# Attention and its end in another order: next pair converted first, reciprocals later, broadcasts behind the tail scores, the first batch's root in three steps

## The chip, the cores and the metric

The kernel runs on one core of one Trainium2 chip. The metric is the device time of one execution in microseconds (us). The kernel before the change took 605.54 us (median of 3 runs, 603.80 to 607.98).

The core's engines run side by side, each through its own list of instructions in order: TensorE (PE, matrix products), VectorE (DVE), ScalarE (ACT), GpSimd (POOL) and SyncE (SP), which issues most transfers (DMA). They meet at semaphores only: an instruction that waits holds up everything behind it on its engine.

## The reference, cut to what matters

Attention with a soft cap, then two gated layers. Every matrix product is made in pieces of higher and lower halves of the operands (`hi`/`lo`), since the result is float32.

```python
# q, k, v: (2 batches, 12 heads, 448 rows, 64 columns)
scores = cap * tanh(matmul(q, k.T) / sqrt(64) / cap)
attn = exp(scores - max(scores))
attn = attn / (sum(attn) + 1e-9)
x = matmul(attn, v)                      # -> (896, 768), heads side by side
rms = sqrt(mean(x * x) + 1e-6)
xn = x / rms * rms_g
h = silu(xn @ w_gate) * (xn @ w_val)     # 768 -> 1536
y = h @ w_out                            # 1536 -> 768
z = y @ w_in                             # 768 -> 2048
out = (max(z, 0) + alpha * min(z, 0)) @ w_out2
```

## The kernel before, in words

The 24 heads are taken as 12 pairs (0 to 5 are the first batch, 6 to 11 the second). A pair is worked on in two bursts of scores, so there are 24 bursts, 0 to 23: burst 2i holds the score groups 0 and 1 of pair i, burst 2i + 1 the groups 2 and 3. For each burst, a list written out by hand gives this order: PE makes the scores (`qk`, L189), ACT takes tanh and exp of them (`soft`, L199 and L201), PE multiplies the preceding burst's exp with V (`pv`, L212), and then come the steps that `at(n, ...)` has hung on this burst, in the order in which they were hung. Every step puts its instructions at the end of its engines' lists. The score banks in PSUM are two, so scores of a burst wait for the tanh of the one before.

The steps that the change touches are:

- `prep` (L175, L176): DVE splits the next pair's Q and K into `hi` and `lo`. `load_raw` and `load_v`: SP issues the loads of a later pair. The tiles for each of them are two.
- `sums` (L228): PE adds up exp over the keys into `us`. `evac_o` (L254) and `evac_u` (L262): DVE copies O and these sums out of PSUM; four small transfers (L267) then spread the sums over partitions (`gt`).
- `recip` (L276 to L287): for two pairs together, DVE makes the reciprocals of the sums in four small instructions, and SP issues two transfers (L287) of their halves `th` and `tl` into rows `r`.
- `norm` (L312, L313): PE broadcasts such a row over the partitions (one matmul into `rps`), and DVE multiplies O by it. `square` (L294 to L302): POOL, or ACT in the last pairs, squares the result and POOL adds the squares up.
- `rms` (L331 to L335): PE sums the squares of a batch over the partitions (`ms`), ACT takes the root, DVE the reciprocal. `xnorm` (L348 to L354): DVE scales a tile by it and, in the first batch, splits it into halves.
- `w_top`, `w_bits`, `w_hi`, `w_lo` (L103, L107, L120, L124): ACT and DVE unpack a weight tile and split it. `sum1` to `sum4` (L115): POOL adds weight tiles. Eight weight tiles are unpacked within the attention.
- `sums_now`, `norm_now`: the same sums and norm for the last pair, without the transfers.
- `product` (L366) and `products` (L378): PE's weight products. Directly behind the attention stand the first four products (`A11` with `B11`, `A12` with `B21`, each for the weight groups 0 and 1, two rows of nine matmuls each), with the rest of the normalisation between them; then the second weight stage begins with `products` into the bank `m`.

In the kernel before, the root of the first batch is one step: root on ACT, reciprocal on DVE, and the weight casts of the same burst behind both. The long rest of the program (the seven products of each weight block, their sums, the second layer) has a list of its own, which the change leaves alone but for one subtraction.

## Time and profile before

| what | value |
|---|---|
| three runs | 603.80, 605.54, 607.98 us |
| profiled execution | 603.23 us, of which the span of the trace is 601.5 us |
| PE busy | 574.0 us, 95% of the span, 2925 matmuls |
| DVE busy | 387.1 us, 64% |
| ACT busy | 340.5 us, 57% |
| POOL busy | 110.1 us, 18% |
| transfers | 66.05 MB, mean 110 GB/s |
| granted clock, mean | 0.994 of full speed |

PE is busy nearly all the time, but not evenly: in the first 150 us there are slices with six to nine tenths, and one whose granted clock is below full speed. The share is an average over stages; what a change in one stage is worth is read from that stage. Names such as `s<-hi,lo` in the rows mean output tile and input tiles. "x8" means that eight instructions stand in one row, and `[4.19 <-ACT pt L199]` that the engine was idle for 4.19 us before the row, until ACT's instruction of L199 on tile `pt`.

### The profile page before, as it was taken

How to read it: one execution, taken by the hardware profiler on the slowest of the kernel's cores; microseconds unless marked ns; L12 is line 12 of the kernel's file. 1: busy time of each engine (PE TensorE's matmuls, PEld its weight loads, DVE VectorE, ACT ScalarE, POOL GpSimd, SP SyncE). 2: the span in 40 equal slices, each digit the busy share in tenths (PEclk: the TensorE clock that was granted, in tenths of full speed). 3: DMA queues.
4: the chain of work that ended last, by engine and by line, in shares of the span. 5: the costliest groups of instructions: out<-in, count | busy, mean ns of one | idle time of the engine just before them, and what ended most of it. 6: DMA issues, size and time to landing. Idle time of an engine off the chain costs nothing.

```text
span 601.5 us, 7318 instructions
## 1 busy us (share of the span) xinstructions
PE 574.0 (95%) x2925; PEld 473.2 (79%) x2925; DVE 387.1 (64%) x428; ACT 340.5 (57%) x389; POOL 110.1 (18%) x60
## 2 busy tenths in 40 slices
PE   6989996999899999999999999999989999999997
PEld 3434332467789999999999999999989889999996
DVE  4546767959899777758861555989986877604100
ACT  6898867834836446347362543686775977323101
POOL 0001550234005524510000035400451000000000
PEclk9999999899999999999999999999999999999999
DMA  7553432040033543313433563003331344431002
GB/s 256 178 175 113 150 103 69 3 158 1 1 106 122 161 146 114 141 53 105 163 134 125 170 244 112 0 1 109 134 125 53 111 152 157 158 129 69 1 1 92
DMA packets 17166, 66.05 MB, mean 110 GB/s; under 512 B 4204, under 2 KB 4716, under 8 KB 17132
## 3 DMA queue, kind: packets, MB, share of 16 engines
q1 hardware_dynamic: 16844, 65.45, 31.6%
q8 instruction: 23, 0.38, 0.2%
q0 software_dynamic: 144, 0.13, 0.1%
q14 instruction: 11, 0.09, 0.0%
q10 hardware_dynamic: 144, 0.00, 0.0%
HBM read 62.66 MB, written 2.75 MB: 109 GB/s over the span
## 4 chain that ended last, share of the span: by engine, by line
PE 74%; DVE 16%; ACT 4%; DMA 3%; issue 2%; SPq 1%; ACTq 0%; DVEq 0%
PE s L366 18%; PE m L366 15%; PE s L633 6%; PE s L629 6%; PE s L631 6%; PE m L629 5%; PE m L633 5%; PE m L631 5%; PE oo L212 2%; DVE b L542 2%; PE s L189 2%; DVE lo L176 2%; DMA gt<-us 2%; DVE wt L107 1%; PE m L378 1%
## 5 line engine op out<-in xcount | busy, mean ns | idle before, releaser
L124 DVE TENSOR_TENSOR wl<-wt,wh 128x768 fp32r<-128x768 f32 x98 | 108.4, 1111 | 94.3 <-ACT wh L120 93.2
L115 POOL TENSOR_TENSOR wt<-wt 128x768 f32<-128x768 f32 x40 | 91.6, 2296 | 250.4 <-DVE wt L107 144.9
L120 ACT CAST wh<-wt 128x768 fp32r<-128x768 f32 x98 | 81.3, 833 | 93.0 <-PE s L631 22.1
L103 ACT CAST top<-raw 128x768 f16<-128x768 bf16 x68 | 72.6, 1076 | 48.3 <-DVE wt L107 40.8
L107 DVE SCALAR_TENSOR_TENSOR wt<-raw,top 128x768 uint32<-128x768 uint32 x68 | 68.2, 1006 | 0.0
L366 PE MATMUL s<-xh,wh 128*128 128x448 f32 x222 | 57.5, 368 | 0.9 <-DVE b L542 0.9
L366 PE MATMUL s<-xl,wh 128*128 128x448 f32 x222 | 57.2, 366 | 0.8 <-DVE xl L542 0.8
L366 PE MATMUL s<-xh,wl 128*128 128x448 f32 x222 | 57.1, 366 | 0.0
L629 PE MATMUL s<-ks,wh 128*128 128x448 f32 x176 | 50.4, 366 | 1.1 <-DVE b L870 1.1
L633 PE MATMUL s<-ks,wl 128*128 128x448 f32 x176 | 50.3, 365 | 0.0
L199 ACT ACTIVATE pt<-s,cinv 128x896 f32<-128x896 f32 (+1 forms) x48 | 41.1, 905 | 12.4 <-PE s L189 12.2
L366 PE MATMUL m<-xh,wh 128*128 128x448 f32 x174 | 45.0, 367 | 2.1 <-ACT b L489 1.5
L629 PE MATMUL m<-ks,wh 128*128 128x448 f32 x160 | 45.5, 366 | 0.5 <-DVE b L542 0.5
L366 PEld LDWEIGHTS s<-xh,wh 128*128 128x128 f32 x222 | 41.5, 188 | 5.1 <-ACT wh L120 1.2
L633 PE MATMUL m<-ks,wl 128*128 128x448 f32 x160 | 45.4, 365 | 0.0
L366 PEld LDWEIGHTS s<-xl,wh 128*128 128x128 f32 x222 | 41.6, 188 | 4.5 <-DVE xl L542 1.2
L366 PE MATMUL m<-xl,wh 128*128 128x448 f32 x174 | 44.7, 365 | 0.0
L366 PE MATMUL m<-xh,wl 128*128 128x448 f32 x174 | 44.7, 365 | 0.0
L366 PEld LDWEIGHTS s<-xh,wl 128*128 128x128 f32 x222 | 41.7, 188 | 3.3
L212 PE MATMUL oo<-pt,vt 128*64 128x448 f32 x192 | 42.2, 561 | 1.9 <-ACT pt L201 1.8
L631 PE MATMUL s<-b,wh 128*128 128x448 f32 x144 | 41.2, 365 | 0.0
L631 PE MATMUL m<-b,wh 128*128 128x448 f32 x144 | 40.9, 365 | 0.0
(136 smaller groups left out, 899.5 us busy)
## 6 DMA issues: line engine op xcount, KB each, us to landing
raw<-w_in SPq DMA_DIRECT2D x68, 768.0 KB, 4.3
rw<-qk_in SPq DMA_DIRECT2D x11, 480.0 KB
vt<-v_in SPq DMA_DIRECT2D x12, 256.0 KB
out<-o SPq DMA_DIRECT2D x5, 448.0 KB
gt<-us SPq DMA_DIRECT2D x44, 1.8 KB, 1.9
out<-o SPq DMA_DIRECT2D x2, 224.0 KB, 2.1
rw<-qk_in SPq DMA_DIRECT2D x1, 256.0 KB
rw<-qk_in SPq DMA_DIRECT2D x1, 224.0 KB
```

The source lines that it names most:

```text
L103: nc.scalar.copy(top_of[u].bitcast(F16)[:, 1::2], raw_t[u].bitcast(BF16)[:, 4:4 * UW + 4:4])
L107: nc.vector.scalar_tensor_tensor(out=f_t[u].bitcast(U32), in0=raw_t.pop(u).bitcast(U32)[:, 1:2 * UW + 1:2], scalar=13, in1=top_of.pop(u), ...
L115: nc.gpsimd.tensor_tensor(out=t, in0=f_t[a], in1=f_t[b], op=op)
L120: nc.scalar.copy(h_t[u], f_t[u].rearrange("p (k m) -> p k m", m=P))
L124: nc.vector.tensor_tensor(out=l_t[u], in0=f_t[u].rearrange("p (k m) -> p k m", m=P), in1=h_t[u], op=ALU.subtract)
L176: nc.vector.tensor_tensor(out=lo[i], in0=r, in1=hi[i], op=ALU.subtract)
L199: nc.scalar.activation(out=t[:, n:n + w], in_=st.pop((i, g))[:, :w, :S], func=AF.Tanh, scale=cinv)
L212: nc.tensor.matmul(oo[i][h * D:h * D + D, :S], vv[:, 2 * c + h, :], t[:, n, :], start=c == 0, stop=c == 3, skip_group_check=True,)
L366: nc.tensor.matmul(ps[:, r, :S], lhs, rhs, start=first and n == 0, stop=n == len(mm) - 1, skip_group_check=True,)
L629: nc.tensor.matmul(dst[l], wh[:, o, :], xh[l], start=first, stop=False)
L631: nc.tensor.matmul(dst[l], wh[:, o, :], xl[l], start=False, stop=False)
L633: nc.tensor.matmul(dst[l], wl[:, o, :], xh[l], start=False, stop=fin)
```

## The change

The instructions stay what they are; only the broadcasts of pairs 9 and 10 go to another PSUM bank (`u`, that of the row sums, instead of `r`). What changes is the order. The list now has two parts for each burst: `ahead` steps run behind the scores and before `soft` and the V product, `at` steps as before.

- `prep` of the next pair comes first in its burst, with its loads, ahead of the sums and copies of the pair before. The copy of the row sums moves one burst forward.
- `recip` comes behind `prep` and behind the loads. `norm` is cut in two: the broadcast and the multiply run ahead of the V product in the odd bursts, `square` at the end of the burst. Pairs 8 and 9, whose norms stood among the products, are now broadcast in the last burst.
- `w_hi` and `w_lo` run at least two bursts behind `w_bits`; `sum3` and one `sum4` on POOL are now within the attention.
- `rms` is cut into `rms_sum` (PE), `rms_root` (ACT) and `rms_tail` (DVE), in bursts 18, 19 and 20 for the first batch. `xnorm` of tiles 0 to 3 follows in bursts 21 to 23, 4 and 5 behind the attention.
- Behind the attention the products are cut into rows, with the last norms, the second root and the S1 halves between them in another order.

```diff
@@ -305,13 +305,12 @@
 
     s2 = {}
 
-    def norm(i):
+    def norm(i, bank="r"):
         b, p = divmod(i, NP)
         n, j = group[i]
-        rps = ps_r.tile([P, 512], F32, tag="r", name="rps")
+        rps = ps_r.tile([P, 512], F32, tag=bank, name="rps")
         nc.tensor.matmul(rps[:, :S], sel_t[:, j, :], r2[n % 2], start=True, stop=True)
         nc.vector.tensor_tensor(out=xf[b][:, p, :], in0=ee.pop(i), in1=rps[:, :S], op=ALU.mult)
-        square(i)
 
     def norm_now(i):
 
@@ -324,14 +323,20 @@
 
     rstd, spare = {}, {}
 
-    def rms(b):
-        ms = ps_o.tile([P, 512], F32, tag="o", name="ms")
+    ms_of = {}
+
+    def rms_sum(b):
+        ms = ms_of[b] = ps_o.tile([P, 512], F32, tag="o", name="ms")
         parts = s2.pop(b)
         for n, t in enumerate(parts):
             nc.tensor.matmul(ms[:, :S], ones, t, start=n == 0, stop=n == len(parts) - 1)
+
+    def rms_root(b):
         spare[b] = xpool.tile([P, K3, S], F32, tag="B22h", name="spare")
         rstd[b] = spare[b][:, 2]
-        nc.scalar.activation(out=rstd[b], in_=ms[:, :S], func=AF.Sqrt, scale=1.0 / DM, bias=rms_b)
+        nc.scalar.activation(out=rstd[b], in_=ms_of.pop(b)[:, :S], func=AF.Sqrt, scale=1.0 / DM, bias=rms_b)
+
+    def rms_tail(b):
         nc.vector.reciprocal(out=rstd[b], in_=rstd[b])
 
 
@@ -419,61 +424,70 @@
         nc.vector.tensor_scalar_mul(eps_t, eps_t, SM_EPS)
 
         bursts = [(i, b) for i in range(NPAIR) for b in range(2)]
-        later = {}
+        early, later = {}, {}
 
         def at(n, fn, *a):
             later.setdefault(n, []).append((fn, a))
 
+        def ahead(n, fn, *a):
+            early.setdefault(n, []).append((fn, a))
+
         NA = len(bursts)
         last = NPAIR - 1
-        for i in range(last):
-            at(2 * i + 2, sums, i)
-            at(2 * i + 3, evac_u, i)
+        conv = conv_seq[:]
+        for u in conv[:RAW]:
+            at(1, w_load, u)
         for i in range(NPAIR):
-            at(2 * i, prep, i + 1)
-            at(2 * i, load_raw, i + 2)
-            at(2 * i, load_v, i + 1)
-            if i < last:
-                at(2 * i + 2, evac_o, i)
-                n, j = group[i]
-                if j == len(members[n]) - 1 and n < len(members) - 1:
-                    at(2 * i + 4, recip, n)
-                    if n < len(members) - 2:
-                        for m, i2 in enumerate(members[n]):
-                            at(2 * i + 6 + m, norm, i2)
-            if i == NP - 1:
-                at(2 * i + 9, rms, 0)
-                for m in range(NP):
-                    at(2 * i + 10 + m * 2 // 3, xnorm, m)
-        for u in conv_seq[:RAW]:
-            at(1, w_load, u)
-        for j, u in enumerate(conv_seq[:]):
-            s0 = 3 + 9 * j // 4
-            at(s0, w_top, u)
-            at(s0 + 1, w_bits, u)
-            if j < len(conv_seq) - RAW:
-                at(s0 + 1, w_next, u)
-            if u[2] in ("A11", "A12"):
-                at(s0 + 1, w_hi, u)
-                at(s0 + 2, w_lo, u)
-            if u[2] == "A22":
-                at(s0 + 1, sum1, "g", u[1])
-                at(s0 + 2, sum2, "g", u[1])
+            e = 2 * i
+            at(e, prep, i + 1)
+            at(e, load_raw, i + 2)
+            at(e, load_v, i + 1)
+            if i > 0:
+                at(e, sums, i - 1)
+                if i % 2 == 1 and i > 2:
+                    at(e, recip, (i - 3) // 2)
+                if i - 2 in range(len(conv)):
+                    at(e, w_bits, conv[i - 2])
+                    if i - 2 < len(conv) - RAW:
+                        at(e, w_next, conv[i - 2])
+                if i == 10:
+                    at(e, rms_tail, 0)
+                at(e, evac_o, i - 1)
+                at(e, evac_u, i - 1)
+            if i in range(3, last):
+                ahead(e + 1, norm, i - 3)
+                at(e + 1, square, i - 3)
+            if i - 1 in range(len(conv)):
+                at(e + 1, w_top, conv[i - 1])
+        for i in (last - 3, last - 2):
+            ahead(NA - 1, norm, i, "ru"[i - last + 3])
+        for n, j in ((6, 0), (8, 1), (18, 6), (22, 7)):
+            at(n, w_hi, conv[j])
+            at(n + 1, w_lo, conv[j])
+        for g in range(2):
+            n = 13 + 2 * g
+            at(n, sum1, "g", g)
+            at(n + 1, sum2, "g", g)
+            at(n + 2, sum3, "g", g)
+        at(20, sum4, "g", 0)
+        at(18, rms_sum, 0)
+        at(19, rms_root, 0)
+        for m in range(4):
+            at((21, 21, 22, 23)[m], xnorm, m)
         for n in range(NA):
             i, b = bursts[n]
             for g in (2 * b, 2 * b + 1):
                 qk(i, g)
+            for fn, a in early.pop(n, []):
+                fn(*a)
             soft(i, b)
             if n > 0:
                 pv(*bursts[n - 1])
             for fn, a in later.pop(n, []):
                 fn(*a)
+        assert not early and not later
         sums_now(last)
         pv(*bursts[-1])
-        for n in sorted(later):
-            if n == NA:
-                for fn, a in later.pop(n):
-                    fn(*a)
 
         def pair_tile(pool, tag):
             return pool.tile([P, 2, 512], F32, tag=tag, name=tag)
@@ -489,32 +503,31 @@
             nc.scalar.copy(home, pa[g][:, :, :S])
 
         nc.scalar.activation(out=cinv, in_=rms_b, func=AF.Sqrt)
-        for n in sorted(later):
-            for fn, a in later.pop(n):
-                fn(*a)
         for g in range(2):
             pa[g] = pair_tile(ps_s, "s")
+        square(last - 3)
+        square(last - 2)
+        xnorm(4)
         recip(len(members) - 1)
         norm_now(last)
-        norm(last - 3)
-        product(pa[0], ("g", 0, "A11"), "B11", True)
-        norm(last - 2)
+        sum4("g", 1)
+        product(pa[0], ("g", 0, "A11"), "B11", True, rows=(0,))
+        norm(last - 1, "u")
+        square(last - 1)
+        product(pa[0], ("g", 0, "A11"), "B11", True, rows=(1,))
+        first_sum(0, ct("c21"))
         w_hi(("g", 0, "S1"))
         w_lo(("g", 0, "S1"))
-        first_sum(0, ct("c21"))
-        for g in range(2):
-            sum3("g", g)
-        product(pa[1], ("g", 1, "A11"), "B11", True)
-        norm(last - 1)
-        for g in range(2):
-            sum4("g", g)
-        product(pa[0], ("g", 0, "A12"), "B21", False, rows=(0,))
+        product(pa[1], ("g", 1, "A11"), "B11", True, rows=(0,))
+        rms_sum(B - 1)
+        rms_root(B - 1)
+        xnorm(5)
+        rms_tail(B - 1)
+        product(pa[1], ("g", 1, "A11"), "B11", True, rows=(1,))
+        first_sum(1, ct("c21"))
         w_hi(("g", 1, "S1"))
-        w_lo(("g", 1, "S1"))
-        rms(B - 1)
-        first_sum(1, ct("c21"))
         c11 = [spare[B - 1][:, :2], xpool.tile([P, 2, S], F32, tag="B22l", name="c11")]
-        product(pa[0], ("g", 0, "A12"), "B21", False, rows=(1,))
+        product(pa[0], ("g", 0, "A12"), "B21", False)
         nc.scalar.copy(c11[0], pa[0][:, :, :S])
         product(pa[1], ("g", 1, "A12"), "B21", False)
         w_hi(("g", 0, "S2"))
@@ -571,6 +584,7 @@
         one, low = tile_maker("T1", i1, x0[:, lo3], x1[:, lo3], x0[:, lo3])
         for k in range(K3):
             one(k)
+        w_lo(("g", 1, "S1"))
         w_hi(("g", 1, "S2"))
 
 
```

**DVE and SP around burst 10**, where pair 6 is converted (`hi`, `lo`), pairs 2 and 3 get their reciprocals (`gf`, `th`, `tl`) and pair 4's O and sums are copied (`ee`, `us`). DVE before:

```order
L313 TENSOR_TENSOR xf<-ee,rps 128x448 [waits PE_49]
L276 SCALAR_TENSOR_TENSOR gf<-gt,eps_t 64x28 [waits DMAHW6_49,DMAHW5_49,DMAHW7_49,DMAHW1_49,DMAHW0_49]
L279 RECIPROCAL gf<-gf 64x28 [waits DVE_49]
L282 CAST th<-gf 64x28 [waits DVE_49]
L283 TENSOR_TENSOR tl<-gf,th 64x28 [waits DVE_49]
L254 COPY ee<-oo 128x448 [waits PE_49]
L175 CAST hi<-rw 128x960 [waits DMAHW2_49]
L176 TENSOR_TENSOR lo<-rw,hi 128x960 [waits DVE_49]
L107 SCALAR_TENSOR_TENSOR wt<-raw,top_91 128x768 [waits DMAHW4_49,Activation_49]
L262 COPY us<-us 128x448 [waits PE_49]
L313 TENSOR_TENSOR xf<-ee,rps 128x448 [waits PE_49]
```

DVE with the change:

```order
L313 TENSOR_TENSOR xf<-ee,rps 128x448 [waits PE_49]
L124 TENSOR_TENSOR wl<-wt,wh 128x768 [waits Activation_49]
L175 CAST hi<-rw 128x960 [waits DMAHW2_49]
L176 TENSOR_TENSOR lo<-rw,hi 128x960 [waits DVE_49]
L276 SCALAR_TENSOR_TENSOR gf<-gt,eps_t 64x28 [waits DMAHW6_49,DMAHW5_49,DMAHW7_49,DMAHW1_49,DMAHW0_49]
L279 RECIPROCAL gf<-gf 64x28 [waits DVE_49]
L282 CAST th<-gf 64x28 [waits DVE_49]
L283 TENSOR_TENSOR tl<-gf,th 64x28 [waits DVE_49]
L107 SCALAR_TENSOR_TENSOR wt<-raw,top_91 128x768 [waits DMAHW4_49,Activation_49]
L254 COPY ee<-oo 128x448 [waits PE_49]
L262 COPY us<-us 128x448 [waits PE_49]
```

SP's issues of the same burst, loads of Q and K (`rw`) and V (`vt`), the reciprocals' two transfers into `r`, a weight load (`raw`) and the first transfer of the row sums (`gt`):

```order
-L287 DMA r_1_89<-th 4x16x28 [waits DMAHW1_49,DVE_49]
-L287 DMA r_1_89<-tl 4x16x28 [waits DMAHW2_49,DVE_49]
-L162 DMA rw<-qk_in 128x960 [waits DMAHW3_49]
-L167 DMA vt<-v_in 128x512 [waits DMAHW4_49,PE_49]
+L162 DMA rw<-qk_in 128x960 [waits DMAHW1_49]
+L167 DMA vt<-v_in 128x512 [waits DMAHW2_49,PE_49]
+L287 DMA r_1_89<-th 4x16x28 [waits DMAHW3_49,DVE_49]
+L287 DMA r_1_89<-tl 4x16x28 [waits DMAHW4_49,DVE_49]
 L93 DMA raw<-w_in 128x3072 [waits DMAHW5_49,DVE_49]
 L267 DMA gt<-us 16x1x28 [waits DMAHW6_49,DVE_49]
```

On DVE the conversion has moved from behind the copy of O, which waits for PE, to the head of the burst; the reciprocal's four instructions stand behind it, and both copies behind these. On SP the two transfers into `r` stood ahead of the two loads and now stand behind them; the load of V waits for PE.

**PE around burst 11**, where the first of these reciprocals is broadcast (`rps`), between the scores of burst 11 and the V product of burst 10:

```order
 L189 MATMUL s<-lo,hi 128x448
-L212 MATMUL oo<-pt,vt 64x448 [waits DMAHW3_49,Activation_49]
+L312 MATMUL rps<-r_1_89,sel_t 128x448 [waits DMAHW4_49,DMAHW3_49,DVE_49]
+L212 MATMUL oo<-pt,vt 64x448 [waits Activation_49]
 L212 MATMUL oo<-pt,vt 64x448 x3
 L189 MATMUL s<-hi 128x448 [waits DVE_49,Activation_49]
...
 L228 MATMUL us<-pt,half 32x448 x2
-L312 MATMUL rps<-r_1_89,sel_t 128x448 [waits DMAHW2_49,DMAHW1_49]
 L189 MATMUL s<-hi 128x448 [waits Activation_49]
```

The broadcast, which waits for transfers, stood behind the row sums of burst 12; it now stands a burst earlier, between scores and V product.

**ACT from burst 19 to 20**, around the root (`spare<-ms`), with tanh and exp (`pt`) of both bursts. Before:

```order
L199 ACTIVATE pt<-s,cinv 128x448 [waits PE_49]
L201 ACTIVATE pt<-pt,cap_t 128x1344 [waits Activation_49]
L334 ACT_TABLE_LOAD
L334 ACTIVATE spare<-ms,rms_b 128x448 [waits PE_49]
L120 CAST wh<-wt 128x768 [waits DVE_49]
L199 ACT_TABLE_LOAD
L199 ACTIVATE pt<-s,cinv 128x896 [waits PE_49] x2
L201 ACTIVATE pt<-pt,cap_t 128x1792 [waits Activation_49]
```

With the change:

```order
L199 ACTIVATE pt<-s,cinv 128x448 [waits PE_49]
L201 ACTIVATE pt<-pt,cap_t 128x1344 [waits Activation_49]
L337 ACT_TABLE_LOAD
L337 ACTIVATE spare<-ms,rms_b 128x448
L199 ACT_TABLE_LOAD
L199 ACTIVATE pt<-s,cinv 128x896 [waits PE_49] x2
L201 ACTIVATE pt<-pt,cap_t 128x1792 [waits Activation_49]
```

The weight cast (`wh<-wt`) between the root and the second table load, which waits for DVE, is gone from there.

## Rows read from the trace of the kernel before

**Rows 1.** Busy time by stretch: start:end, length, busy time of each engine, clock, DMA, GB/s

```profile
16.10:99.28 83.18, 77.49 (x490) 32.57 (x488) 48.14 (x69) 68.82 (x65) 20.24 (x14) 1.00 0.41 134
99.28:144.55 45.27, 38.52 (x195) 23.40 (x193) 37.65 (x51) 25.78 (x30) 14.35 (x9) 0.92 0.16 59
102.25:105.61 3.36, 0.04 (x2) 0.04 (x2) 3.22 (x7) 3.21 (x4) 0.00 (x0) 0.66 0.00 0
```

**Rows 2.** PE in order of time, bursts 2 to 4: start, duration, instructions, idle before

```profile
16.10 1.32 PE L228 MATMUL us<-pt,ones 128*32 128x448 f32 x10
...
17.74 0.47 PE L189 MATMUL s<-hi 64*128 64x448 f32 x2
...
19.35 1.73 PE L212 MATMUL oo<-pt,vt 128*64 128x448 f32 x8
21.00 0.47 PE L189 MATMUL s<-hi 64*128 64x448 f32 x2
...
22.41 1.72 PE L212 MATMUL oo<-pt,vt 128*64 128x448 f32 x8
24.06 1.32 PE L228 MATMUL us<-pt,ones 128*32 128x448 f32 x10
```

**Rows 3.** Chain of work that ended last, 43 to 139 us: start, duration, what

```profile
...
43.95 0.41 PE rps L312
...
133.49 1.85 PE s L366 x9
135.35 2.25 PE ms L331 x6
...
```

**Rows 4.** PE in order of time from pair 10 to the second weight stage

```profile
105.57 0.74 PE L189 MATMUL s<-hi 64*128 64x448 f32 x2 [4.19 <-ACT pt L199]
...
119.17 2.42 PE L239 MATMUL us<-pt,ones 128*64 128x448 f32 x12
...
122.18 1.67 PE L212 MATMUL oo<-pt,vt 128*64 128x448 f32 x8
...
144.55 1.09 PE L378 MATMUL m<-xh,wh 128*128 128x448 f32 x4 [1.46 <-ACT xh L562]
```

**Rows 5.** ACT and DVE in order of time around the first batch's root

```profile
95.18 1.42 ACT L201 ACTIVATE pt<-pt,cap_t 128x1344 f32<-128x1344 f32 x1
...
96.61 1.28 ACT L334 ACT_TABLE_LOAD   x1
...
97.91 0.63 ACT L334 ACTIVATE spare<-ms,rms_b 128x448 f32<-128x448 f32 x1
98.57 2.95 DVE L335 RECIPROCAL spare<-spare 128x448 f32<-128x448 f32 x1 [3.77 <-ACT spare L334]
...
102.37 0.83 ACT L120 CAST wh<-wt 128x768 fp32r<-128x768 f32 x1 [3.83 <-DVE wt L107]
...
103.22 1.28 ACT L199 ACT_TABLE_LOAD   x1
```

**Rows 6.** DVE by operation, from answers on single tiles: duration in ns min/median/max

```profile
L175 DVE CAST hi<-rw x11: 640/650/1080, 7.2 to 106.7; 128x960 fp32r<-128x960 f32 x11
L176 DVE TENSOR_TENSOR lo<-rw,hi x11: 1157/1159/1987, 7.9 to 107.8; 128x960 fp32r<-128x960 f32 x11
...
L313 DVE TENSOR_TENSOR xf<-ee,rps x11: 602/615/623, 44.4 to 133.5; 128x448 f32<-128x448 f32 x11
...
L282 DVE CAST th<-gf x6: 168/172/1510, 33.2 to 123.8; 64x28 fp32r<-64x28 f32 x5, 32x28 fp32r<-32x28 f32 x1
```

**Rows 7.** SP's transfer of reciprocals, and the row sums' time to landing

```profile
L287 SPq DMA_DIRECT2D r<-tl x6: 588/598/679, 34.3 to 124.9; - x6
...
DMA to landing us min/median/max: 1.7/1.9/5.3
```

**Rows 8.** POOL and DVE in order of time, 70 to 75 us

```profile
70.27 3.75 POOL L115 TENSOR_TENSOR wt<-wt 128x768 f32<-128x768 f32 x2
...
72.54 1.51 DVE L282 CAST th<-gf 64x28 fp32r<-64x28 f32 x1
```

## The prediction, made before the changed kernel ran

> **What bounds the kernel now.** I read the busy time by stage first, then TensorE's (PE's) order of time in the attention stage, then the other engines' rows at PE's gaps. After the attention PE is hardly ever idle, and the order of instructions there is unchanged. So two stretches decide, both marked by PE events that exist before and after the change: A, from the first pair's row sums to those of pair 9 (83.18 us), and B, from there to the first product of the second weight stage (45.27 us, granted clock 0.92) [rows 1].
>
> PE's own work in A: without a wait, one head pair takes 24.06 - 16.10 = 7.96 us, of which row sums 1.64, odd-burst scores 1.61, probabilities times V 1.65, even-burst scores 1.41 and again 1.65 [rows 2]. A broadcast of reciprocals adds 0.41, the root's sums of three tensors take 2.25, so of two 1.50, and one row of a weight product 1.85 [rows 3]. A holds 9 pairs (71.64), 6 broadcasts (2.46) and the first batch's sums (1.50): 75.60 of work, so 7.58 us of waits. B holds two row sums (3.28), two odd and one even scores (4.63), three V products (4.95), the last sums (122.18 - 119.17 = 3.01) and V product (1.67), five broadcasts (2.05), eight product rows (14.80), the second batch's sums (2.25) and the 1.46 at its end: 38.10 of 45.27, so 7.17 more of waits [rows 2 to 4].
>
> What the waits in B are: one of 4.19 us for ScalarE (ACT), and behind it matmuls that take 0.74 instead of 0.47 us, at the lower of the two clock levels [rows 2, 4]. ACT made PE wait thus: exp ends at 96.60, a table load and the root follow, then ACT idles 3.83 us, since the weight cast behind the root waits for VectorE (DVE), which first runs the root's 2.95 us reciprocal; then comes the second table load and only then the next tanh [rows 5].
>
> **The change, part by part.**
>
> *Next pair converted first.* DVE's `hi` and `lo` (0.65 + 1.16 us) [rows 6] no longer stand behind the copy of O, which waits for PE; they start once the preceding score burst has freed their buffers, a whole pair before PE needs them. PE's waits on them go. The input load they need was issued a pair earlier; its landing is not shown, so this is bounded by nothing gained (the load is late instead) and all of it.
>
> *Weight casts later.* They now read what DVE made at least one pair earlier. ACT no longer waits in line for DVE; I cost the moved casts at nothing, as they fit the gap that ACT has today. The copy of the row sums and its four transfers move a burst forward, so that the reciprocals find them landed; nothing waits for them sooner. All of A's 7.58 us then disappears, if nothing replaces it.
>
> *Root in three steps.* Behind the root, ACT goes straight to the second table load: the 3.83 and the cast of 0.83 leave the path, 4.66 against a PE wait of 4.19 [rows 4, 5], so 0 to 1.0 remains; I take 0.3. The slow matmuls go with the wait. The 2.95 us reciprocal now stands ahead of the two copies of pair 9; the next row sums need one of these about 8 us later, so it costs nothing there.
>
> The Trainium skill weighs in here. The rows show exp ending at 96.60, the load starting at 96.61 and the root at 97.91, when the load of 1.28 ends: nothing else lies there [rows 5]. *ScalarE: Activation LUTs*, "What ACT_TABLE_LOAD costs", states besides the load a drain of about 1.38 us for each switch to another set. By the page the two switches would cost 2.8 us more than the sum has. By the rows they cost 2 x 1.28, as summed.
>
> *Broadcasts behind the scores.* This adds a wait. Let R be a broadcast's start on PE. The next one is due at R + 7.96 + 0.41 = R + 8.37. DVE reaches the reciprocal after the broadcast (0.41), the norm multiply (0.61), `hi`, `lo`, and needs about 1.0 for four small operations (one of them 0.17) [rows 3, 6]: R + 3.8. But SyncE's queue (SP) now issues the two transfers of the reciprocals behind the load of V, which waits for PE's V product at R + 0.41 + 1.65 + 1.41 + 1.65 = R + 5.12. With an issue of at most 0.6 for V (as the transfers' own) and 0.6 for the first transfer, the second starts at R + 6.3. Its landing has no row; the nearest is the row sums' small transfer, 1.7 to 5.3, median 1.9 [rows 7]. I take 1.9, since 5.3 is far from the median: R + 8.2, just in time. Behind the waiting broadcast PE has the V product and all after it, so a late landing is paid in full.
>
> DVE is not always on time. GpSimd (POOL) holds it up: two POOL sums start at 70.27 and end at 74.02, and DVE's small cast between them lasts 1.51, to 74.05 [rows 8]; unhindered it is 0.17, and `hi` and `lo` have maxima of 1.08 and 1.99 [rows 6]. I price the reciprocal's first step, which reads two tiles as `lo` does, like that cast. The change brings squares and two weight sums (1.9 us each) right into the pair before burst 15: 0.41 + 0.61 + 1.08 + 1.99 + 1.51 + 0.3 + 1.51 = 7.4, and 0.2 to 1.9 for the low half; its transfer starts at R + 7.6 to 9.3 and lands at 9.5 to 11.2, against 8.37: 1.1 to 2.8, I take 1.9. Burst 7 (no POOL work): 0.3, bounds 0 and 0.7. Burst 11 (squares only): 0.7, bounds 0 and 1.3. Burst 19, where POOL's sums run out and PE has 1.50 more to do: 0.7, bounds 0 and 2.0. Burst 23 has the root's reciprocal and two normalised tiles (3.36 us together, [rows 1]) ahead on DVE: bounds 0 and 2.3, I take 1.2. The odd one at the tail, for pair 10: DVE needs from burst 23 on 0.41, two multiplies, a weight subtraction, two more tiles and the reciprocal, about 7; two issues and the landing make R + 9.3 to 10.3; PE arrives after two broadcasts, a V product, last sums, last V product and a product row at R + 9.0: 0.3, bounds 0 and 1.3.
>
> *Tail.* One broadcast leaves B for A. The eight product rows, now taken one row at a time, cost what they did. The second root still waits for the squares of pairs 10 and 11, which are ready before PE comes to sum them; its reciprocal and the three difference tiles end before ACT's last copy, which the 1.46 at the end of B hangs on as before. Weight sums on POOL that moved earlier gain nothing: no PE wait hung on them. DVE's moved subtraction of the second S1 has the first half of the next product to hide behind; without that cover about 1 us.
>
> **The sum.** A: 71.64 + 7 x 0.41 + 1.50 = 76.0, and 0.3 + 0.7 + 1.9 + 0.7 = 3.6 of waits: 79.6. B: 38.10 - 0.41 = 37.7, and 0.3 + 1.2 + 0.3 = 1.8: 39.5. Together 119.1 against 128.45: **9.3 us less**. The profiled execution took 603.23 (span 601.5 and 1.73 around it), so 593.9; it lies 2.31 below the median of the three runs, and from the median the forecast is **596.2**. With no wait at all the gain is 14.75 (590.8), with every upper bound (11.4 of waits) 3.3 (602.2).
>
> **Rivals.**
>
> 1. *The reciprocals land in time.* POOL and DVE fall out of step, no wait but small ones (up to 3.5 in all): 591 to 594. For it: the clean chain lands 0.2 early. Against it: the small cast that sat out a whole POOL sum. Chance 0.18.
>
> 2. *The broadcast's wait takes the place of the waits removed*, so that the change does not do what it says: 7 to 11 us in all, near my upper bounds, 599 to 602, take 601. For it: PE's order leaves 0.2 us to spare. Against: only two of six broadcasts have heavy POOL work near. Chance 0.20.
>
> 3. *Slower: the transfers' landing.* If the reciprocals land like the slowest row-sum transfer, 5.3 instead of 1.9, six broadcasts wait 3.4 more each: 20.4 + 5.4 - 14.75 = 11 slower, and such waits bring the lower clock back: B at 0.92 lost up to 3.6 us by it [rows 1]. That is 617 to 620. It decides from a mean wait of 14.75 / 6 = 2.5 us per broadcast. For it: V's load of 256 KB goes out just ahead on the same queue. Against: the median of 1.9, and that the larger weight loads are now issued behind the reciprocals. Chance 0.05.
>
> 4. *Each table switch costs more than its load.* Two more pauses of ACT between bursts 19 and 20 would hold the next V product about 2.5 us longer: 598.7. The rows leave no place for a pause [rows 5]. Chance 0.05. By the drain of *ScalarE: Activation LUTs* in the Trainium skill it is this time.
>
> **How the numbers follow.** My forecast (594 to 599) has 0.52. The range 590 to 602.5 takes in it, rivals 1 and 4, and most of rival 2; its ends are the sums without waits and with all of them. About 1% (6 us, so 599.5 here) is what a measurement can tell from no change. Faster by more: forecast, rival 1, half of rival 4, little of rival 2: 0.73. Within: 0.22. Slower: rival 3, 0.05.
>
> **What would show it.** Right: ACT without idle time before weight casts in the attention; no PE wait of over 1 us for tanh behind the root; A near 79.6 and B near 39.5 with a clock of 1.00; PE's longest waits at broadcasts for the reciprocals' transfers, above all at bursts 15 and 23. The step on landing is wrong if no broadcast waits, or if all do by 3 us. The step on POOL is wrong if the small casts of the reciprocals stay at their short time there. The whole is wrong if A's length hardly falls or if `hi` waits for its load, or if the time that B gives up comes back as PE waits after its end.

## The result and the profile after the change

The changed kernel took 601.52 us (median of 14 runs, 596.84 to 605.23), the kernel before beside it 607.69: ratio 0.9895, 95% interval 0.9860 to 0.9929. That is 6.2 us less where 9.3 were forecast. 601.52 lies in the range of 590 to 602.5, near its upper end, and outside the 594 to 599 that the prediction took as its likeliest. (It reckoned from 605.54 for the kernel before; the 607.69 beside it is the median of more runs, so the differences are compared here.) Between the two profiled executions the gain is 603.23 - 596.84 = 6.4. All times are medians of all runs; ratios and intervals leave out the few slow runs, those over 1.5% above the fastest of their kernel. Busy time by stretch after the change, with the columns of [rows 1], for stage A, stage B and all that follows:

```profile
16.13:93.44 77.31, 75.62 (x490) 32.65 (x488) 57.91 (x70) 69.29 (x66) 31.89 (x18) 1.00 0.46 144
93.44:138.14 44.70, 37.57 (x195) 23.49 (x193) 37.56 (x49) 24.91 (x30) 7.42 (x5) 0.96 0.16 60
138.14:595.10 456.96, 447.37 (x2196) 411.65 (x2196) 294.14 (x291) 235.29 (x283) 74.62 (x32) 1.00 0.31 105
```

A fell from 83.18 to 77.31 (forecast 79.6). B fell from 45.27 only to 44.70 (forecast 39.5) [rows 1]. What follows took 456.95 before (144.55 to 601.5) and 456.96 now: nothing comes back there. PE in order of time, with the waits that the trace names in the two stages (in brackets the idle time before the row and what ended it); the only other one is the 1.46 for ACT that closes B, as in [rows 4]:

```profile
35.60 0.44 PE L312 MATMUL rps<-r,sel_t 128*128 128x448 f32 x1 [0.22 <-DMA r<-tl]
...
43.85 0.36 PE L312 MATMUL rps<-r,sel_t 128*128 128x448 f32 x1
...
52.97 0.44 PE L312 MATMUL rps<-r,sel_t 128*128 128x448 f32 x1 [0.77 <-DMA r<-tl]
...
70.28 0.44 PE L312 MATMUL rps<-r,sel_t 128*128 128x448 f32 x1 [0.70 <-DVE wt L107]
...
97.85 1.72 PE L212 MATMUL oo<-pt,vt 128*64 128x448 f32 x8 [0.74 <-ACT pt L201]
...
107.06 0.65 PE L312 MATMUL rps<-r,sel_t 128*128 128x448 f32 x2 [1.18 <-DMA r<-tl]
...
119.64 0.50 PE L312 MATMUL rps<-r,sel_t 128*128 128x448 f32 x1 [3.72 <-DMA r<-tl]
119.94 1.32 PE L371 MATMUL s<-xh,wh 128*128 128x448 f32 x3
```

The product rows behind the longest wait, as stretches with the columns of [rows 1] (the clock is the third number from the end):

```profile
119.94:123.30 3.36, 3.36 (x10) 2.98 (x9) 1.84 (x3) 1.10 (x2) 0.00 (x0) 0.50 0.93 380
123.30:125.14 1.84, 1.84 (x10) 1.71 (x9) 0.00 (x0) 1.63 (x2) 0.00 (x0) 1.00 1.02 427
```

The reader is to see three things. The wait for ACT behind the root (4.19 in [rows 4]) has shrunk to 0.74. The small waits are at broadcasts, bursts 7, 11, 15 and 23. (At burst 15 the trace names DVE's L107, which the broadcast does not read and which ended 0.11 us before it; the second transfer of its reciprocals had been issued at 68.17, 2.1 us before.) And one new wait, 3.72 us at 119.64, for the reciprocals of pair 10, is nearly as long as the one removed, with slow matmuls behind it: one product row takes 3.36 us at a granted clock of 0.50, the next 1.84 at 1.00. Why that transfer was late stands in DVE's and POOL's rows in order of time:

```profile
109.48 0.68 DVE L353 SCALAR_TENSOR_TENSOR xf<-xf,g_t,spare 128x448 f32<-128x448 f32 x1
...
110.23 2.83 POOL L302 TENSOR_TENSOR s<-s,sq 128x448 f32<-128x448 f32 x2 [8.87 <-ACT sq L300]
110.62 1.44 DVE L359 TENSOR_TENSOR xl<-xf,xh 128x448 fp32r<-128x448 f32 x1
111.98 1.56 DVE L353 SCALAR_TENSOR_TENSOR xf<-xf,g_t,spare 128x448 f32<-128x448 f32 x1
113.02 2.21 POOL L115 TENSOR_TENSOR wt<-wt 128x768 f32<-128x768 f32 x1
113.58 1.91 DVE L358 CAST xh<-xf 128x448 fp32r<-128x448 f32 x1
115.52 0.62 DVE L359 TENSOR_TENSOR xl<-xf,xh 128x448 fp32r<-128x448 f32 x1
116.06 0.23 DVE L276 SCALAR_TENSOR_TENSOR gf<-gt,eps_t 32x28 f32<-32x28 f32 x1
```

The two normalised tiles ahead of the reciprocals (109.48 to 116.06) hold three operations that took 1.44, 1.56 and 1.91 us instead of 0.62, 0.68 and 0.39: 3.2 us lost, beside POOL's adds and weight subtraction.

### The profile page after: what moved, and what is told of

It reads as the page before. It is cut to its first block, busy times and chain, and to the rows that moved or that the text cites. A ratio compares the mean times of both kernels' runs of the same rounds, so it can differ in the third digit from the quotient of the medians.

```text
span 595.1 us, 7323 instructions
## 1 busy us (share of the span) xinstructions
PE 571.0 (96%) x2925; PEld 473.2 (80%) x2925; DVE 398.0 (67%) x428; ACT 340.2 (57%) x389; POOL 114.8 (19%) x60
## 4 chain that ended last, share of the span: by engine, by line
PE 79%; DVE 12%; DMA 4%; issue 2%; ACT 1%; SPq 1%; ACTq 0%; DVEq 0%
PE s L371 19%; PE m L371 15%; PE s L647 6%; PE s L643 6%; PE s L645 6%; PE m L643 5%; PE m L647 5%; PE m L645 5%; PE oo L212 3%; PE s L189 3%; DVE b L555 2%; PE us L228 2%; DMA r<-tl 1%; PE m L383 1%; DVE wl L124 1%
## 5 line engine op out<-in xcount | busy, mean ns | idle before, releaser
L124 DVE TENSOR_TENSOR wl<-wt,wh 128x768 fp32r<-128x768 f32 x98 | 106.6, 1093 | 94.4 <-ACT wh L120 93.3
L107 DVE SCALAR_TENSOR_TENSOR wt<-raw,top 128x768 uint32<-128x768 uint32 x68 | 71.3, 1051 | 1.7 <-ACT top L103 1.3
```

Source lines behind the costliest of these rows:

```text
L107: nc.vector.scalar_tensor_tensor(out=f_t[u].bitcast(U32), in0=raw_t.pop(u).bitcast(U32)[:, 1:2 * UW + 1:2], scalar=13, in1=top_of.pop(u), ...
L124: nc.vector.tensor_tensor(out=l_t[u], in0=f_t[u].rearrange("p (k m) -> p k m", m=P), in1=h_t[u], op=ALU.subtract)
```

## The experiments

Each run is an edit of the changed kernel (e6, e10 and e12: of the kernel before). A and B are the stages of its profiled execution, "after B" the rest of its span; the time is the median, with the kernel before beside it on the same chip.

| run | A | B | after B | time (before) | ratio, 95% interval |
|---|---|---|---|---|---|
| before | 83.18 | 45.27 | 456.95 | 607.69 | 1 |
| changed | 77.31 | 44.70 | 456.96 | 601.52 (607.69) | 0.9895 [0.9860, 0.9929] |
| e1 | 77.46 | 42.77 | 461.6 | 600.20 (605.13) | 0.9917 [0.9885, 0.9948] |
| e2 | 77.43 | 43.25 | 461.5 | 596.00 (605.13) | 0.9858 [0.9821, 0.9895] |
| e3 | 77.91 | 42.99 | 462.2 | 599.31 (605.13) | 0.9891 [0.9853, 0.9929] |
| e4 | 77.28 | 40.11 | 459.4 | 594.45 (605.13) | 0.9814 [0.9784, 0.9844] |
| e5 | 77.61 | 45.95 | 457.0 | 598.50 (607.17) | 0.9876 [0.9829, 0.9923] |
| e6 | 84.90 | 44.65 | 461.8 | 608.70 (607.17) | 1.0006 [0.9960, 1.0052] |
| e7 | 77.92 | 45.08 | 461.8 | 603.27 (607.17) | 0.9954 [0.9919, 0.9988] |
| e8 | 78.38 | 47.13 | 457.1 | 602.07 (607.17) | 0.9942 [0.9902, 0.9981] |
| e9 | 76.74 | 40.23 | 461.5 | 596.02 (606.80) | 0.9845 [0.9807, 0.9883] |
| e10 | 84.44 | 43.21 | 457.6 | 604.89 (606.80) | 0.9983 [0.9957, 1.0010] |
| e11 | 76.25 | 41.29 | 459.5 | 597.64 (606.38) | 0.9856 [0.9801, 0.9911] |
| e12 | 75.89 | 42.42 | 462.2 | 596.59 (606.38) | 0.9817 [0.9759, 0.9875] |

The 16 to 18 us ahead of A stand in no column. The part after B has the same number of matmuls in all and yet takes 457 to 462 us; the last section shows where. So steps of 1 or 2 us are read from A and B, and the medians only say whether a whole kernel gained. A and B are of one execution each: e1 to e4 leave A as it is, and theirs lie between 77.28 and 77.91, so steps of 0.6 or less are within the spread.

### The tail: e1 to e4

e1:
```
+        recip(len(members) - 1)
         xnorm(4)
-        recip(len(members) - 1)
         norm_now(last)
```


> Only the four small steps of pair 10's reciprocals go ahead of the fifth normalised tile on DVE. Stretch B of the changed kernel is 44.70 us, of which 3.72 is PE's wait for this transfer and about 1.5 the matmuls behind it at the lower clock. Theory (the tile in front of the reciprocals makes them late): PE reaches the broadcast at about 115.9 and finds the data, as first step to broadcast took 3.58 us (116.06 to 119.64) and now starts near 112.0. But DVE has as much to do before the last pair's own 2.95 us reciprocal as before, so the squares of pairs 10 and 11 stay at 121.46 to 122.56, and PE, some 5 us earlier at the second batch's sums, waits about 2.5 us there: B about 41.4 to 42.4, whole time 2.3 to 3.3 less than the changed kernel. Rival (SP's queue or the transfer's landing sets the wait, not DVE's order): the wait stays above 3 us, B 44.4 to 45.0. Rival (nothing else is late, the wait was all): B 39.5.

e2:
```
         norm_now(last)
-        sum4("g", 1)
...
         square(last - 1)
+        a12, s2g = ("g", 1, "A12"), ("g", 1, "S2")
+        nc.vector.tensor_tensor(out=f_t[a12], in0=f_t[a12], in1=f_t[s2g], op=ALU.subtract)
+        f_t["g", 1, "S4"] = f_t[a12]
```


> The second weight subtraction S4, on POOL at 113.02 to 115.23 in the changed kernel, is done by DVE instead, behind the multiplication of pair 10 where DVE idled 3.29 us. DVE's order is else unchanged. Theory (POOL's sums hold DVE's tile up): the fifth normalised tile takes 1.7 us instead of 4.1 (111.98 to 116.06), the reciprocals start near 113.7, the broadcast near 117.2 after a wait of about 1.3; the squares of pairs 10 and 11 end near 120.2 and PE does not wait for them; B 40.8 to 42.3. Rival (POOL has no part, the tile was slow by itself): fifth tile still about 4 us, B 44.4 to 45.0. Rival (landing): B unchanged too, but with a tile of 1.7 us and a wait that ends no sooner.

e3:
```
-        xnorm(4)
         recip(len(members) - 1)
         norm_now(last)
...
         square(last - 1)
+        xnorm(4)
```


> Pair 10's reciprocals and the whole normalisation of pair 11 go ahead of the fifth normalised tile on DVE; the tile moves behind the multiplication of pair 10. It is first needed by a product that PE starts about 14 us later. Theory (order on DVE, with the last pair's chain as the next limit): no wait at pair 10's broadcast (0 to 0.5), squares of pair 11 near 118.5, no wait over 0.5 at the second batch's sums, no matmuls at the lower clock behind it, so B 39.5 (39.2 to 40.5), the forecast of stage B as it was made; whole time about 5 less than the changed kernel. Rival (landing or SP's queue): wait above 3 us, B 44.4 to 45.0. Rival (B ends on the three difference tiles and ACT's casts, whatever goes before): B above 42.

e4 is e3 and e2 together.


> The order of the run before (reciprocals and the last pair first) and also the weight subtraction S4 on DVE instead of POOL. Theory: once the fifth tile is out of the way the order alone suffices, since no step of pair 10 or 11 is held up by POOL by more than 1 us: B within 0.5 of the run before (39.2 to 40.5). Rival (POOL also holds up the last pair's chain): B 0.5 to 2 less than in the run before, and that run then shows a wait at the second batch's sums. Rival (landing): B 44.4 to 45.0.

The wait at pair 10's broadcast was 1.81 in e1, 2.28 in e2, 1.81 in e3 and 0.66 in e4. The rival that the landing sets it is out: the wait moves with DVE's order. But e1 and e3 were to bring it to nothing, and missed; they gained 1.9 and 1.7 us of B instead of 2.3 to 3.3 and about 5. e2 was to leave 1.3 of it and left 2.28. DVE and POOL in e3, in order of time, show why:

```profile
110.96 2.84 POOL L302 TENSOR_TENSOR s<-s,sq 128x448 f32<-128x448 f32 x2 [8.88 <-ACT sq L300]
112.73 1.11 DVE L276 SCALAR_TENSOR_TENSOR gf<-gt,eps_t 32x28 f32<-32x28 f32 x1
113.77 1.83 POOL L115 TENSOR_TENSOR wt<-wt 128x768 f32<-128x768 f32 x1
113.88 0.32 DVE L279 RECIPROCAL gf<-gf 32x28 f32<-32x28 f32 x1
114.23 1.40 DVE L282 CAST th<-gf 32x28 fp32r<-32x28 f32 x1
```

Put first, the reciprocals' small steps meet the same POOL work: the step at 112.73 ends 0.04 behind POOL's adds (113.80), the cast at 114.23 ends 0.03 behind POOL's subtraction (115.60). The reciprocal between them, with one input and no change of type, takes its 0.32 while POOL runs. So an operation of DVE is not slowed in proportion; it sits out POOL's instruction, whatever its own size. The Trainium skill says so in *SBUF — State Buffer*, "Who interferes with whom": DVE and GpSimd share a port pair that one instruction holds to its end, and among DVE's operations copies and casts can ask for it, and those with two inputs in SBUF do. The rows agree, the reciprocal included.

Order alone is worth 1.7 of B, the subtraction off POOL alone 1.45, both 4.6 (44.70 to 40.11): either alone leaves part of the delay. In e3 the first step and the cast are held up, as shown; in e2 the fifth tile still stands ahead of the reciprocals, and its first operation takes 1.56 us beside POOL's adds. With both, the slow matmuls are gone too (clock of B 1.00; 0.96 in the changed kernel and in e1 to e3), 1.5 of the 4.6. The theory of e4, that order suffices, is wrong. Its rival is right that POOL holds up more, but not where it said, on the last pair's chain; and it is 2.9 us rather than 0.5 to 2. The limit behind it that e1 expected, the squares of the last pairs, was never reached: no run waits at the second batch's sums.

### The first root: e5 and e6

e5:
```
-                if i == 10:
-                    at(e, rms_tail, 0)
...
         at(19, rms_root, 0)
+        at(19, rms_tail, 0)
```


> The changed kernel with one thing undone: the first root's 2.95 us reciprocal on DVE again stands straight behind the root, at burst 19, instead of a burst later. Theory (what made ACT wait was the weight cast behind the root, and it is gone from there in the changed kernel): ACT goes from the root to the table load and tanh without idling, B 44.70 changes by at most 0.5, A by at most 0.5. Rival (the split itself took the wait away, as the sum of the forecast credited it): a PE wait of 3 to 4.2 us for ACT behind the root and slow matmuls after it, A and B together 3 to 7 longer.

e6, in the kernel before (`rms_tail` is the reciprocal, taken out of `rms`):
```
                 at(2 * i + 9, rms, 0)
+                at(2 * i + 10, rms_tail, 0)
...
         rms(B - 1)
+        rms_tail(B - 1)
```


> The kernel before with one thing done: the first root's reciprocal moves one burst later on DVE, nothing else moves; the weight cast stays behind the root on ACT. Theory (DVE's 2.95 us stood ahead of what the cast waits for): ACT's idle of 3.83 us behind the root shrinks to under 1, PE's wait of 4.19 to under 1.2, the matmuls behind it stay at the higher clock, B 45.27 becomes 38.5 to 42; A unchanged (83.0 to 83.4). Rival (the reciprocal a burst later holds up the copies of the next pair instead): PE waits about as long one pair later, B 44 to 46. Rival (table loads, not the cast): B unchanged.

In e5 the V product behind the root waits 0.75, as in the changed kernel: the 4.19 does not come back when the split is undone. B is 1.25 longer, more than the 0.5 allowed but far from the rival's 3 to 7: DVE idles 2.47 us for the root ahead of the reciprocal, all behind it is later, and the broadcast at burst 23 waits 2.23 for its transfer, with matmuls at the lower clock behind it (clock of B 0.93), and pair 10's waits 2.34. In e6 ACT indeed goes through without idling:

```profile
100.17 0.63 ACT L334 ACTIVATE spare<-ms,rms_b 128x448 f32<-128x448 f32 x1
100.70 0.82 ACT L120 CAST wh<-wt 128x768 fp32r<-128x768 f32 x1
101.55 1.28 ACT L199 ACT_TABLE_LOAD   x1
```

against the 3.83 in [rows 5]. Yet B falls only by 0.6, and the kernel is no faster. PE's waits in B of e6 (in total, times, longest):

```profile
PE rps L312 <- DVE us L320: 1.9, 1, 1.9
PE oo L212 <- ACT pt L201: 1.0, 1, 1.0
PE s L189 <- ACT pt L201: 0.8, 1, 0.8
PE s L189 <- DVE lo L176: 0.6, 1, 0.6
PE s L189 <- ACT pt L199: 0.3, 1, 0.3
```

These come to 4.5, against 4.19 and 0.99 in the kernel before. So the first rival holds (B 44 to 46), though in several waits and not in one: the wait is handed on. (A of e6 is 1.7 longer than before for matmuls at the lower clock behind the waits for `hi` and `lo` at burst 16, clock 0.98.)

### Stage A: e7, e10 and e12

e7:
```
-            at(e, prep, i + 1)
             at(e, load_raw, i + 2)
...
                 at(e, evac_o, i - 1)
+            at(e, prep, i + 1)
+            if i > 0:
                 at(e, evac_u, i - 1)
```


> The changed kernel with one thing undone: DVE converts the next pair behind the copy of O again, not ahead of it. Theory (the early conversion took away the waits for hi and lo, which the trace of before names with 2.8 of the 7.58 us in A, the rest being ACT's): A 77.31 becomes 78.3 to 80.1, with PE waits for hi or lo near POOL's sums; the rest of A's gain stays. Rival (the whole gain of A came from the conversion): A 82 to 83.5. Rival (the weight casts alone did it): A within 0.5 of 77.31.

e10, in the kernel before:
```
+        for j, u in enumerate(conv):
+            at(2 * j + 3, w_top, u)
+            at(2 * j + 4, w_bits, u)
...
+        for n, j in ((6, 0), (8, 1), (18, 6), (22, 7)):
+            at(n, w_hi, conv[j])
+            at(n + 1, w_lo, conv[j])
+        for g in range(2):
+            at(13 + 2 * g, sum1, "g", g)
+            at(14 + 2 * g, sum2, "g", g)
```


> The kernel before with one thing done: the weights' bits, casts and sums of the attention stage in the changed kernel's bursts (S3 and S4 stay in the tail); the order of conversion, reciprocals, broadcasts, root and tail is that of before. Theory (the casts' place, not the early conversion, gives A its gain, and no cast stands behind the root any more): A 83.18 becomes 76.5 to 79, no PE wait for ACT; behind the root a PE wait of under 1.2 instead of 4.19, B 45.27 becomes 39.5 to 42.5. Rival (the gain of A needs broadcasts, row-sum copies and conversion together): A 81 to 83.5. Rival (the split of the root is needed for B): B above 44.

e12, e10 and also:
```
+        for i in range(NPAIR):
+            at(2 * i, prep, i + 1)
         for i in range(last):
             at(2 * i + 2, sums, i)
...
-            at(2 * i, prep, i + 1)
             at(2 * i, load_raw, i + 2)
```


> The tenth run (the kernel before with the weights' casts and sums in the changed kernel's bursts) with the next pair's conversion also ahead of the copies on DVE. Theory (casts take away ACT's waits, and with the reciprocals and broadcasts still in the old order the early conversion takes away the waits for hi and lo, 3.6 us in the tenth run with the slow matmuls behind the longest): A 84.44 becomes 75.7 to 78, the two parts alone make A's gain. Rival (hi and lo are late for POOL, wherever they stand): waits for hi or lo stay above 2 us, A above 80.

e10 moves more than the casts: the weights' loads, bits and first sums on POOL go with them. It missed twice: A is 84.44, longer than before and than either of its ranges, and B, 43.21, lies between its two. PE does not wait for ACT any more, neither in A nor behind the root, but it waits for DVE, and drops to the lower clock behind the longest such wait (PE in order of time):

```profile
75.75 0.47 PE L189 MATMUL s<-hi 64*128 64x448 f32 x2 [2.02 <-DVE hi L175]
76.85 0.74 PE L189 MATMUL s<-hi,lo 64*128 64x448 f32 x2 [0.62 <-DVE lo L176]
...
79.02 3.25 PE L212 MATMUL oo<-pt,vt 128*64 128x448 f32 x8
```

In e12 those go too. Its stretches, and all of PE's waits in them but the 1.46 that closes B (in total, times, longest):

```profile
16.45:92.34 75.89, 75.89 (x489) 32.69 (x487) 50.57 (x67) 70.31 (x67) 22.08 (x14) 1.00 0.45 145
92.34:134.76 42.42, 37.95 (x196) 22.85 (x194) 35.76 (x51) 23.74 (x29) 14.36 (x9) 0.96 0.18 63
```

```profile
PE rps L312 <- DVE xf L313: 1.9, 1, 1.9
PE rps L312 <- DVE us L320: 1.0, 1, 1.0
```

A of 75.89 is close to the 75.60 of work that the prediction summed for the old order, with its six broadcasts, and no wait is left. Two parts of the change make all of A's gain: the weights' steps in their new bursts, and the early conversion. e12 has the old order of broadcasts, copies, root and tail, and its A + B is 118.31 against 122.01 of the whole change. e7 shows that in the changed kernel the early conversion is worth 0.6 at most: there, without it, PE never waits for `hi` or `lo`; a broadcast waits longer instead (1.51 at burst 15 in place of 0.70). Its 77.92 lies between the ranges of its theory and of its last rival, so neither is shown.

### The broadcasts: e8, e9 and e11

e8 (and the same for the two broadcasts of burst 23):
```
-                ahead(e + 1, norm, i - 3)
+                at(e + 1, norm, i - 3)
```


> The changed kernel with the broadcasts of bursts 7 to 23 put behind the product with V again (1.65 us later on PE); all else as changed. Theory (these broadcasts wait only for a transfer that is a little late): the waits of 0.22, 0.77 and 0.70 in A and of 1.18 at burst 23 go, A 75.5 to 76.0; pair 10's wait in the tail stays or grows by up to 1, B 43.3 to 44.8; in all 1.5 to 3 us less than the changed kernel. Rival (behind V they hold up the next scores, since ACT's exp is then late for V): PE waits for ACT in place of the waits removed, A 77 to 79, no gain.

e9, e4 and also:
```
+            if i % 2 == 1 and i > 2:
+                at(e, recip, (i - 3) // 2)
             at(e, prep, i + 1)
...
                 at(e, sums, i - 1)
-                if i % 2 == 1 and i > 2:
-                    at(e, recip, (i - 3) // 2)
```


> The tail of the fourth run (reciprocals and last pair first, S4 on DVE), and in the attention each pair of reciprocals goes ahead of the next pair's conversion on DVE and its transfers ahead of the loads of the next inputs on SP. Theory (the broadcasts wait because DVE's conversion and, at burst 7, V's load stand ahead of the reciprocals; POOL holds up what is left at burst 15): the waits at bursts 7 and 11 go, that at burst 15 falls below 0.5, A 77.28 becomes 75.7 to 76.4; at burst 23 the row sums' own transfers land only near the time DVE gets there, so 0.5 to 1.2 stays, B 39.0 to 40.2; in all 1 to 2.5 us below the fourth run. Rival (the row sums' landing is as late as the reciprocals' turn on DVE already): waits as before, and DVE idles ahead of the reciprocals, so that hi and lo come late: A 77 to 78.5.

e11, e9 and also:
```
-            n = 13 + 2 * g
+            n = 15 + 2 * g
```


> The ninth run with the weights' sums on POOL two bursts later (S1 of the first block at burst 15 instead of 13, and so on), so that none runs beside the reciprocals ahead of burst 15. Theory (what is left of the wait at burst 15, 1.53 us, is two small steps of the reciprocals held up by POOL's sums, 1.28 and 1.51 us instead of 0.23 and 0.17): the wait at burst 15 falls below 0.4 and A from 76.74 to 75.3 to 76.2; at burst 19, where POOL now sums, PE's 1.50 us of root sums cover most, at most 0.8 of wait; B as in the ninth run (39.8 to 40.6). Rival (the row sums' landing sets it): wait at burst 15 over 1.2, A 76.4 to 77.

e8 gained nothing and lost 1.07 in A and 2.43 in B, so its theory is wrong. The wait at burst 11 is 0.63, nearly the 0.77 of the changed kernel:

```profile
45.30 0.47 PE L312 MATMUL rps<-r,sel_t 128*128 128x448 f32 x1
...
54.40 0.44 PE L312 MATMUL rps<-r,sel_t 128*128 128x448 f32 x1 [0.63 <-DMA r<-tl]
```

From one broadcast to the next it is 9.10 us here and 9.12 in the changed kernel (43.85 to 52.97). The wait closes a loop: broadcast, norm multiply, a weight's low half, conversion, reciprocals, transfer, broadcast. On DVE in the changed kernel:

```profile
44.25 0.62 DVE L313 TENSOR_TENSOR xf<-ee,rps 128x448 f32<-128x448 f32 x1 [1.16 <-PE rps L312]
44.79 0.95 DVE L124 TENSOR_TENSOR wl<-wt,wh 128x768 fp32r<-128x768 f32 x1
45.66 1.39 DVE L175 CAST hi<-rw 128x960 fp32r<-128x960 f32 x1
47.08 1.98 DVE L176 TENSOR_TENSOR lo<-rw,hi 128x960 fp32r<-128x960 f32 x1
```

Moving every broadcast by 1.65 us moves its whole loop. Only the wait at burst 7, the first broadcast, ahead of which no loop lies, is gone in e8. A lies in the range of the rival (77 to 79), but PE waits for ACT only once in it, 0.49 us; each broadcast costs 0.41 there (45.30 to 45.71) and 0.29 ahead of V (43.85 to 44.14). e9 shortens the loop instead, and the waits at bursts 7 and 11 are gone; that at burst 15 grew to 1.53, so A fell by 0.5 only, less than expected and within the spread. (e9 moves the reciprocals on DVE and their transfers on SP at once. In the changed kernel V's load was the later at burst 7, issued at 32.18 with DVE done at 31.67, and DVE at burst 11, 50.00 against 48.99.) DVE and PE there:

```profile
63.51 1.28 DVE L276 SCALAR_TENSOR_TENSOR gf<-gt,eps_t 64x28 f32<-64x28 f32 x1 [2.79 <-DMA gt<-us]
...
65.18 1.51 DVE L282 CAST th<-gf 64x28 fp32r<-64x28 f32 x1
...
69.57 0.44 PE L312 MATMUL rps<-r,sel_t 128*128 128x448 f32 x1 [1.53 <-DVE wt L107]
```

Two small steps wait for POOL's sums again, and DVE had idled for the row sums before. With the sums two bursts later (e11) burst 15 does not wait; at burst 19 PE waits 0.29 before the broadcast and 0.24 behind it, and A is 76.25. But the broadcast at burst 23 starts at 106.45, as in e9 (106.41): DVE works without a pause from burst 19 to those reciprocals, so PE, early, waits 2.25 instead of 1.19, the clock falls (0.96), and B is 1.06 longer.

The largest gains over the kernel before beside them are those of e9 (10.8 us), e4 (10.7) and e12 (9.8); only e4's interval lies wholly below that of the changed kernel. e12's A with e4's tail would be 116.0 for A and B; that was not run.

## Why the forecast was right and wrong, step by step

**Right: where the time is.** Only A and B changed. The work of A holds: 75.6 was summed for the old order, and e12 shows 75.89 without a wait; 76.0 for the new one, and the changed kernel shows 77.31 - 1.69 = 75.6. Nearly all of the 7.58 of waits could go: e12 lies 7.29 below the kernel before.

**Waits in A: forecast 3.6, measured 1.69.** Burst 7 came as worked out, 0.22 (0.3). Burst 11, 0.77 (0.7), and, in B, burst 23, 1.18 (1.2, the middle of wide bounds), came out right in part by luck: DVE's chain ahead of burst 11 holds a weight's low half of 0.95 us that the working left out. Burst 15, 0.70 (1.9), and burst 19, none (0.7), were sized too large. At burst 15 the mechanism was there (first step 0.91, cast 1.39, `lo` 1.77 us), but from R = 61.22 DVE was done at 67.64, R + 6.4, where I had added every maximum to 7.6 to 9.3.

**Root: forecast 0.3, measured 0.74; credited to the wrong part.** I let the split take away 4.66 us. The cast's move does it (e10, e5); the split alone hands the wait on (e6).

**The step that failed: the wait at the tail's broadcast, "The odd one at the tail, for pair 10", taken as 0.3 with bounds 0 and 1.3.** It measured 3.72, 3.4 more, and the matmuls at the lower clock behind it cost 3.36 - 1.84 = 1.5, for which the sum had nothing: 4.9 of the 5.2 by which B missed (44.70 - 39.5). The root's 0.74 instead of 0.3 more than makes up the rest. For DVE I wrote "about 7" from burst 23 on; it was 10.0 (107.06 to 117.06). POOL's hold-ups of 3.2 us make up the difference. I had priced these in A and not in the tail, where the same diff puts POOL's weight subtraction, and ACT's squares release POOL's adds, right beside the two tiles. e2 to e4 show it by taking them apart. PE came to this broadcast 8.9 us behind burst 23 (9.0 was forecast), and from DVE's end to the broadcast it took 2.6 (2.3 to 3.3): only DVE's part was wrong. Without this term the sum for B holds to 0.3 us. A's error of 2.3 goes the other way, hence 6.4 instead of 9.3 between profiles; that 601.52 still lies in the range is in part luck.

**Rivals.** Rival 1 is out: the waits at broadcasts came to 6.6, where it allowed 3.5 in all. Rival 2 (601, chance 0.20) gives the time that was measured, and its kind of wait: 6.6, or 8.1 with the slow matmuls, against its 7 to 11. It had all of them near their upper bounds, though; the five in the attention came to 2.9, and the one in the tail alone to nearly three times its bound of 1.3. Rival 3 is out: the last transfer landed in 1.95 us at burst 23 and in 1.80 in the tail. Rival 4 is out, by ACT's rows after the change:

```profile
89.39 1.42 ACT L201 ACTIVATE pt<-pt,cap_t 128x1344 f32<-128x1344 f32 x1
90.82 1.28 ACT L337 ACT_TABLE_LOAD   x1
92.12 0.63 ACT L337 ACTIVATE spare<-ms,rms_b 128x448 f32<-128x448 f32 x1
92.77 1.28 ACT L199 ACT_TABLE_LOAD   x1
94.06 1.91 ACT L199 ACTIVATE pt<-s,cinv 128x896 f32<-128x896 f32 x2
```

From exp's end (90.81) to tanh (94.06) there are two loads and the root, and no pause. The drain that *ScalarE: Activation LUTs* of the Trainium skill states under "What ACT_TABLE_LOAD costs" does not show here.

**Why PE waited 0.8 us longer for `hi` in e10 than before.** Counted from the start of A, `hi` was ready 1.4 us earlier (57.83 against 59.26), but PE, no longer held up by ACT, came 2.2 us earlier (its V product at 54.24 against 56.45). DVE had idled 4.29 us for the row sums' transfer, which stands ahead of `hi` in its list; in e12 `hi` stands ahead of it.

**Open.** e7 and e12 leave a choice of how much of the conversion's worth lies in DVE's order and how much in the clock.

## What to carry to other kernels

When an edit puts a short chain (reciprocals, a small transfer, a broadcast) behind other work on an engine, price every operation ahead of it with the neighbour that can hold it up, in every stage where the chain occurs, and not only where a trace happened to show it. A wait that closes a loop is not shortened by moving its end; shorten the loop. Undo parts one at a time before crediting a gain: here two simple parts took more off A and B than the whole.

## What the runs showed of the hardware

PE shows two paces at a granted clock of 1.00. Groups of three matmuls of the same product follow each other every 0.61 us in the changed kernel, and every 0.62 in e1, for some 240 us:

```profile
179.83 0.77 PE L371 MATMUL m<-xh,wh 128*128 128x448 f32 x3
180.44 0.77 PE L371 MATMUL m<-xh,wl 128*128 128x448 f32 x3
```

```profile
178.21 0.78 PE L371 MATMUL m<-xh,wh 128*128 128x448 f32 x3
178.83 0.78 PE L371 MATMUL m<-xh,wl 128*128 128x448 f32 x3
```

2% of 240 us is 4.8, about the 4.7 us by which the part after B of these two differs, and the times of one kernel spread by nearly twice that (596.84 to 605.23). No run here says what sets it.
